# Retention attention, a routed expert layer and a gated convolution layer on one core: decodings spread evenly over the experts, routing's small products moved by a chunk, one product moved from GpSimd to VectorE

## The chip, the cores and the metric

The kernel runs on one core of one Trainium2 chip, in a single launch. The metric is the device time of that launch in microseconds (us). TensorE multiplies matrices, VectorE and ScalarE (DVE and ACT in the rows) move and change data, GpSimd (POOL) does some products and issues the gathers, and SyncE (SP) only issues transfers. Each engine takes its own instructions strictly in the order in which they stand, and waits for the others by semaphores.

## The reference

Three layers follow one another on a batch of 2 sequences of 768 tokens, 8 heads of 64 (512 features together).

```python
# 1. attention with a decaying state, for each head h
state = gamma[h] * state + outer(k[t], v[t]);   y[t] = scale * q[t] @ state
# 2. one expert of 8 for each token, chosen in sequence
fresh = argmax(logits[b, s])
e = fresh if s == 0 or local_gate[b, s] < 0.5 else prev_e
out[b, s] = softmax(logits[b, s])[e] * (relu(x[b, s] @ w1[e]) @ w2[e])     # 512 -> 1024 -> 512
# 3. a gated layer with a convolution of 3 taps along the sequence
h = relu(x @ w_in);   conv = sum_k conv_w[k] * shifted(h, k)
out = (h * sigmoid(conv)) @ w_out                                          # 512 -> 1024 -> 512
```

The weights of layer 3 (`w_in`, `conv_w`, `w_out`) arrive as 64-bit floats; the rest is 32-bit.

## The kernel before

**Attention** runs over 12 chunks of 128 tokens (6 a sequence), the loop over `i` at the end of `tile_kernel`. A chunk is a fixed row of steps on TensorE: `a_Z` (the state times q), `a_AV` (the masked scores times v), `a_S` (the next chunk's scores; VectorE then masks them into `A`), `a_U` (the state's update), `a_X` (the transposition of the result, with the router's logits) and `a_store`. The inputs of a chunk are loaded three chunks ahead by SyncE and scaled two ahead by GpSimd.

**Routing** decides which tokens go to which expert. It works on groups of chunks (`GROUPS`: three of 3, one of 2, one of 1) and has five parts, a generator `route(g)` that `part(g)` moves on by one: (1) seven small VectorE operations, (2) a transposition and a running maximum, (3) transpositions back and the one-hot matrix `OH`, (4) counting products and the slot rows `sl`, (5) products that put each token's number into its expert's slot (a region of the bank `state`, which `a_U` also writes). In the loop, `due` is the group that ended a chunk ago and `late` the one that ended two ago. `first_gather` fetches the tokens of expert 0's first 128 slots (`x0`) as soon as they are final: `floor0` fills up expert 0's first 128 slots after chunk 9 (`FIRST`), so that later tokens go to the second half.

**The experts** (`moe`). An expert has up to 256 slots. To keep 32-bit accuracy, each operand is split into a high and a low part, and three products replace one; VectorE and ScalarE split the weights unit by unit (`split_unit`: 128x1024, cast `whi` on ScalarE, difference `wlo` on VectorE), eight units an expert, some ten units ahead of their use. Experts 1 to 6 run as `L1` (first product, 4 steps `dt`), `T` (transposition of the next expert's tokens) and `L2` (second product, 4 steps `j`). The first and the last expert run as two halves of 128 slots, `alone`: 8 steps of the first product (f = 0, 1), after each f a `relu` into `hr` and a transposition back (`back(f)`), then 8 steps `ft` of the second. The caller puts work between the steps, numbered n.

**Decoding.** The 64-bit weights of layer 3 are turned into 32-bit ones while the experts run: 16 decodings of 128x512. `dec_first` has ScalarE read the raw tile `draw` (2 buffers) into `dmf` (magnitude and fraction; L217 and L218). `dec_second` has VectorE do five operations (L220 to L226) and GpSimd two (L228, L229), and then issues the load for the decoding after next (`dec_load`). `dec_first` first finishes what is open. The tile `dmf` and the tile `hr` of `alone` share one tag with two buffers (`tag="ow", bufs=2`). `MORE` gives experts 2, 3 and 4 three decodings each; expert 0 has one, experts 1, 5 and 6 two each, and the last one's second part stands in expert 7's first half, at n == 2.

**Layer 3** (`moe2`) alternates `h2` (first product of 386 columns, 12 products each block of 128 features, then `conv` on ScalarE, VectorE and GpSimd) and `o2` (second product).

Everything is emitted in program order (`manual_schedule`): no scheduler moves it.

Of the kernel before, what the change touches and what calls it, by code (L numbers as in the profile page):

```python
# [22 lines left out]
E = 8  # L23
# [11 lines left out]
FIRST = 9  # L35
# [11 lines left out]
MORE = (2, 3, 4)  # L47
# [13 lines left out]
def _consts():  # L61

    if _CONST:
# [24 lines left out]
        "floor0": np.broadcast_to(P * (np.arange(E) == 0), (P, E)),  # L88
        "floor1": np.broadcast_to(P * (np.arange(E) == E - 1), (P, E)),
# [12 lines left out]
def tile_kernel(ctx: ExitStack, tc: tile.TileContext, consts, qk, kv, w1, w2, w_in, conv_w, w_out, out):  # L102
# [336 lines left out]
    def route(g):  # L439
# [49 lines left out]
        if b == FIRST:  # L489

            ve.tensor_tensor(out=c_, in0=end, in1=cv("floor0"), op=ALU.max)
        elif b == NC:


            up = small([P, E], "up8")
            ve.tensor_tensor(out=up, in0=end, in1=cv("thr"), op=ALU.is_gt)
            ve.scalar_tensor_tensor(out=up, in0=up, scalar=float(P), in1=end, op0=ALU.mult, op1=ALU.add)
            ve.tensor_tensor(out=c_, in0=up, in1=cv("floor1"), op=ALU.max)
        else:
            ve.tensor_copy(c_, end)  # L500
# [78 lines left out]
    def transposed(x, hi, lo):  # L579
        p_ = bank("a")  # L580
# [17 lines left out]
    def first_T():  # L598
        xs0[:] = [dp.tile([P, KD, P], F32R, name="xs0", tag=tag) for tag in ("ds", "df")]
        transposed(x0, *xs0)  # L600

    def moe(mo):
# [86 lines left out]
        def L1(e):  # L689
# [3 lines left out]
            for dt in range(KD):  # L693
                wh, wl = split[e * 8 + dt]
                if dt == 0:
                    dec_second(nc.gpsimd)
# [22 lines left out]
        def L2(e):  # L719
# [3 lines left out]
            for j in range(KF // 2):  # L723
                wh, wl = split[e * 8 + KD + j]
                if j == (0 if e in MORE else 1):
                    dec_second(nc.gpsimd)
                    if e in MORE:
                        dec_first(mo)
                elif j == 2:
                    next(rest, None)  # L730
                elif j == 3:
                    dec_second(nc.gpsimd)
                    dec_first(mo)
# [19 lines left out]
        g3, g4 = len(GROUPS) - 2, len(GROUPS) - 1  # L753
        next(first)
# [16 lines left out]
        for n, _ in enumerate(first):  # L771
# [4 lines left out]
            if n == 4:  # L776
                overflow(mo)
        for n, _ in enumerate(alone(0, 1, True)):
            if n == 4:
                dec_first(mo)  # L780
            elif n == 9:
# [14 lines left out]
        for n, _ in enumerate(alone(e, 0, False)):  # L796
            if n == 2:
                dec_second(nc.gpsimd)
# [150 lines left out]
    def moe2(fo):  # L949
# [30 lines left out]
        def conv(c, ft, pb):  # L980
# [13 lines left out]
            nc.gpsimd.tensor_tensor(out=sg, in0=sg, in1=tap[1], op=ALU.mult)  # L994
# [77 lines left out]
    with tc.manual_schedule():  # L1072
# [22 lines left out]
        for i in range(NT):  # L1095
# [14 lines left out]
            part(late)  # L1110
# [4 lines left out]
            a_scale_q(i + 2, nc.gpsimd)  # L1115
            if not last_tile:
                a_S(i + 1)
            part(due)
            part(late)
            if i == FIRST + 1:  # L1120
                first_gather()
            a_U(i)
# [21 lines left out]
            if last_tile:  # L1144
                part(due)
                first_T()
# [57 lines left out]
```

## Time and profile before

| | |
|---|---|
| device time, median of 3 runs | 442.8 us (442.79, 442.8, 444.75) |
| profiled execution: its time, its span | 438.87 us, 436.8 us |
| TensorE busy | 404.5 us, 93% |
| VectorE, ScalarE, GpSimd busy | 296.2, 238.7, 164.5 us |
| mean granted TensorE clock | 0.975 of full speed |

How to read it: the span goes from the first to the last instruction of the profiled execution, and its own time is 2 us above that. In the table of stretches, a row names a stretch in us from the span's start, its length, the busy time and the number of instructions of each engine, the granted clock (1.00 is full speed, 0.50 half) and the share of the 16 DMA engines. In the table of waits, a row names the engine and instruction that waited, who released it, the sum, the number of times and the longest.

### The profile page before, as it was taken

The page shows a single profiled execution, that of the slowest core. Times are in us where ns is not written, and L with a number is a line of the kernel's source. Part 1 is how long each engine was busy: PE and PEld are TensorE (multiplying, and loading weights), DVE is VectorE, ACT ScalarE, POOL GpSimd, SP SyncE. Part 2 cuts the span into 40 slices and gives each one's busy share as a digit, 9 for nine tenths or more (in the row PEclk, how much of TensorE's full clock was granted, in tenths as well). Part 3 has the DMA queues.
Part 4 walks back from the last instruction along what each step waited for, and adds up shares of the span by engine and source line. Part 5 has one row for each costly group of instructions (what it writes and reads, how often), then busy time and mean ns, then how long its engine had stood idle before and what let it go on. Part 6 is the DMA issues. An engine that isn't in the chain of part 4 may idle for free.

```text
span 436.8 us, 7275 instructions
## 1 busy us (share of the span) xinstructions
PE 404.5 (93%) x2771; PEld 348.5 (80%) x2771; DVE 296.2 (68%) x485; ACT 238.7 (55%) x444; POOL 164.5 (38%) x143
## 2 busy tenths in 40 slices
PE   7998887899999995998979999969999999999996
PEld 3876675679989884896958987649987979998976
DVE  2377775649997959779797773576991633994250
ACT  2455542557666447285375752657865635883341
POOL 4644430210436425464464432503950300552030
PEclk9999998999999996999989999989999999999999
DMA  8999983477878768777697701311301001001001
GB/s 294 319 330 368 347 322 122 122 263 215 285 248 287 262 208 281 220 235 244 227 321 237 278 0 48 122 49 48 102 20 50 24 26 49 2 0 43 30 0 72
DMA packets 27974, 73.36 MB, mean 168 GB/s; under 512 B 2977, under 2 KB 3361, under 8 KB 27938
## 3 DMA queue, kind: packets, MB, share of 16 engines
q1 hardware_dynamic: 17490, 47.32, 31.8%
q0 software_dynamic: 4256, 14.68, 11.2%
q10 hardware_dynamic: 6192, 10.88, 6.7%
q8 instruction: 22, 0.36, 0.3%
q14 instruction: 14, 0.11, 0.1%
HBM read 62.39 MB, written 10.49 MB: 167 GB/s over the span
## 4 chain that ended last, share of the span: by engine, by line
PE 40%; DVE 23%; DMA 16%; issue 8%; ACT 7%; POOL 5%; SPq 0%; POOLq 0%; ACTq 0%; DVEq 0%
PE c L1022 11%; DVE wlo L185 6%; PE b L970 6%; DMA x<-scr,perm 6%; PE c L740 5%; DMA draw<-in_moe_w_out_dram 4%; PE rt L970 3%; DVE cs L989 3%; DVE gl L999 3%; ACT whi L177 2%; PE x L400 2%; PE sc L341 2%; POOL dmf L228 2%; POOL wdec L229 2%; PE xp L371 2%
## 5 line engine op out<-in xcount | busy, mean ns | idle before, releaser
L185 DVE TENSOR_TENSOR wlo<-raw,whi 128x1024 fp32r<-128x1024 f32 x64 | 85.1, 1347 | 26.9 <-ACT whi L177 26.6
L177 ACT CAST whi<-raw 128x1024 fp32r<-128x1024 f32 x64 | 66.5, 1055 | 23.6 <-PE c L740 14.5
L994 POOL TENSOR_TENSOR sg<-sg,hs 128x384 f32<-128x384 f32 x32 | 37.4, 1169 | 92.1 <-ACT sg L993 92.0
L228 POOL TENSOR_TENSOR dmf<-dmf,ds 128x512 f32<-128x512 f32 x16 | 29.9, 1867 | 93.9 <-DVE ds L226 65.9
L989 DVE SCALAR_TENSOR_TENSOR cs<-hs,cw,cs 128x384 f32<-128x384 f32 x64 | 43.9, 687 | 30.8 <-ACT cs L987 29.6
L740 PE MATMUL c<-whi,hh 128*128 128x512 f32 x96 | 40.2, 419 | 7.0 <-ACT hh L711 7.0
L740 PE MATMUL c<-wlo,hh 128*128 128x512 f32 x96 | 39.6, 412 | 0.0
L999 DVE TENSOR_TENSOR gl<-sg,gh 128x384 fp32r<-128x384 f32 x32 | 34.4, 1076 | 4.6 <-ACT gh L998 4.6
L1022 PE MATMUL c<-whi,gh 128*128 128x512 f32 x88 | 35.1, 399 | 0.8 <-ACT os L1036 0.8
L970 PE MATMUL b<-x,whi 128*128 128x386 f32 x168 | 35.8, 344 | 0.0
L1022 PE MATMUL c<-whi,gl 128*128 128x512 f32 x88 | 35.0, 397 | 0.1
L740 PE MATMUL c<-whi,hl 128*128 128x512 f32 x96 | 31.6, 412 | 3.6 <-DVE hl L712 3.6
L1022 PE MATMUL c<-wlo,gh 128*128 128x512 f32 x88 | 34.7, 394 | 0.0
L970 PEld LDWEIGHTS b<-x,whi 128*128 128x128 f32 x168 | 30.6, 194 | 0.1
L740 PEld LDWEIGHTS c<-whi,hh 128*128 128x128 f32 x96 | 19.3, 201 | 11.6 <-ACT hh L711 7.5
L229 POOL TENSOR_TENSOR wdec<-dmf 128x512 f32<-128x512 f32 x16 | 27.6, 1727 | 1.3
L706 PE MATMUL b<-xsh,wlo 128*128 128x256 f32 x96 | 27.1, 283 | 0.0
L706 PE MATMUL b<-xsh,whi 128*128 128x256 f32 x96 | 27.0, 281 | 0.0
L706 PE MATMUL b<-xsl,whi 128*128 128x256 f32 x96 | 26.8, 279 | 0.0
L740 PEld LDWEIGHTS c<-whi,hl 128*128 128x128 f32 x96 | 18.7, 199 | 9.3 <-DVE hl L712 5.6
L217 ACT ACTIVATE dmf<-draw 128x512 f32<-128x512 f32 x16 | 10.8, 676 | 27.8 <-DMA draw<-in_moe_w_out_dram 16.9
L610 POOL DMA_INDIRECT xg<-scr,permi x15 | 16.8, 1122 | 23.9 <-DVE nbi L541 13.7
(212 smaller groups left out, 1017.4 us busy)
## 6 DMA issues: line engine op xcount, KB each, us to landing
raw<-in_moe_w_dram SPq DMA_DIRECT2D x64, 512.0 KB, 5.1
qk<-in_qk_dram SPq DMA_DIRECT2D x11, 512.0 KB, 6.7
kv<-in_kv_dram SPq DMA_DIRECT2D x11, 512.0 KB, 5.3
scr<-ys ACTq DMA_DIRECT2D x16, 256.0 KB, 4.2
draw<-in_moe_w_out_dram POOLq DMA_DIRECT2D x8, 512.0 KB, 4.4
draw<-in_moe_w_in_dram POOLq DMA_DIRECT2D x6, 512.0 KB, 5.3
scr<-xo ACTq DMA_DIRECT2D x11, 256.0 KB, 6.6
out_dram<-os ACTq DMA_DIRECT2D x11, 256.0 KB, 2.0
```

Of the source, the lines that this page charges most:

```text
L177: nc.scalar.copy(hi, raw[u])
L185: engine.tensor_tensor(out=lo, in0=t, in1=hi.bitcast(F32), op=ALU.subtract)
L228: nc.gpsimd.tensor_tensor(out=f, in0=f, in1=s.bitcast(F32), op=ALU.mult)
L229: nc.gpsimd.tensor_tensor(out=out, in0=f, in1=a.bitcast(F32), op=ALU.add)
L610: nc.gpsimd.indirect_dma_start(out=t, out_offset=None, in_=xrow, in_offset=bass.IndirectOffsetOnAxis(ap=permi[:, col:col + 1], axis=0))
L706: nc.tensor.matmul(o, lhsT=a[:, fs], rhs=b_[:, dt, :], start=(dt == 0 and n == 0 and ft % 2 == 0), stop=(dt == KD - 1 and n == 2), skip_gr ...
L740: nc.tensor.matmul(yp[t], lhsT=a[:, ft, t * P:(t + 1) * P], rhs=b_[:, ws], start=(ft == 0 and a is hh and b_ is wh), stop=(ft == KF - 1 an ...
L970: nc.tensor.matmul(pb[:, 0:WN], lhsT=split[u_in + dt][wi][:, fs], rhs=x_[dt // 2][:, dt % 2, :], start=(n == 0), stop=(n == 3 * KD - 1))
L989: nc.vector.scalar_tensor_tensor(out=cs, in0=tap[j], scalar=cw[:, j, ft:ft + 1], in1=cs, op0=ALU.mult, op1=ALU.add)
L994: nc.gpsimd.tensor_tensor(out=sg, in0=sg, in1=tap[1], op=ALU.mult)
L999: nc.vector.tensor_tensor(out=gl, in0=sg, in1=gh.bitcast(F32), op=ALU.subtract)
L1022: nc.tensor.matmul(ops[t][:, 0:n_], lhsT=a[:, ts_], rhs=b_[:, ws], start=(ft == 0 and n == 0), stop=(ft == KF - 1 and n == 2))
```

## The change

Five things are done. (1) Decodings go to a schedule of two an expert: three start in expert 0 (the first in its first half, into the tiles `dmag` and `df`), two in each of the experts 1 to 6, and the last in expert 7's first half, at n == 6, with its second part at n == 13. (2) Their loads are issued by SyncE, the queue of the experts' weights, instead of GpSimd. (3) Routing's parts 2, 4 and 5 stand later in the loop: part 2 behind `a_U`, part 4 behind `a_AV`, part 5 one chunk later; the last two groups' parts are interleaved anew with expert 0's first steps. (4) `FIRST` becomes 6: expert 0's first 128 slots take tokens of the first sequence alone, `first_gather` stands in chunk 8 instead of 10, and the transposition of `x0` (`first_T`) stands before the last chunk's `a_X` and uses a bank of the scores. (5) The product of the sigmoid with h (L994) goes from GpSimd to VectorE.

```diff
-FIRST = 9
+FIRST = NC
-MORE = (2, 3, 4)
...
-        if b == FIRST:
-            ve.tensor_tensor(out=c_, in0=end, in1=cv("floor0"), op=ALU.max)
-        elif b == NC:
+        if b == NC:
...
-            ve.tensor_tensor(out=c_, in0=up, in1=cv("floor1"), op=ALU.max)
+            ve.tensor_tensor(out=c_, in0=up, in1=cv("floor"), op=ALU.max)
...
-        transposed(x0, *xs0)
+        transposed(x0, *xs0, sc2[:, 0])
...
                 if dt == 0:
-                    dec_second(nc.gpsimd)
+                    dec_second()
...
-                if j == (0 if e in MORE else 1):
-                    dec_second(nc.gpsimd)
-                    if e in MORE:
-                        dec_first(mo)
+                if j == 1:
+                    dec_second()
                 elif j == 2:
                     next(rest, None)
                 elif j == 3:
-                    dec_second(nc.gpsimd)
                     dec_first(mo)
...
         next(first)
+        part(g3)
+        next(first)
         part(g4)
         part(g3)
...
+            if n == 7:
+                dec_first()
         for n, _ in enumerate(alone(0, 1, True)):
-            if n == 4:
+            if n in (3, 12):
                 dec_first(mo)
-            elif n == 9:
+            if n == 9:
...
         for n, _ in enumerate(alone(e, 0, False)):
-            if n == 2:
-                dec_second(nc.gpsimd)
+            if n == 6:
+                dec_first(mo)
+            if n == 13:
+                dec_second()
...
-            nc.gpsimd.tensor_tensor(out=sg, in0=sg, in1=tap[1], op=ALU.mult)
+            nc.vector.tensor_tensor(out=sg, in0=sg, in1=tap[1], op=ALU.mult)
...
             a_Z(i)
-            part(late)
             a_AV(i)
             if i in SPLIT_STEPS:
                 split_first()
             a_load_qk(i + 3)
             a_scale_q(i + 2, nc.gpsimd)
+            part(late)
             if not last_tile:
                 a_S(i + 1)
-            part(due)
-            part(late)
-            if i == FIRST + 1:
+            else:
+                part(due)
+                first_T()
+            part(ends.get(i - 2))
+            a_U(i)
+            if i == FIRST + 2:
                 first_gather()
-            a_U(i)
+            if not last_tile:
+                part(due)
```

The file of the changed kernel is two lines shorter here, so its line numbers are 2 lower up to routing, and up to 6 lower in the experts.

**Routing in the attention loop, on TensorE**, from the counting products (`rt<-cnt`) of the group that ends at chunk 6 or 9. Before, one chunk's products and scores, and then at once the slot products:

```order
L485 LDWEIGHTS sel
L485 MATMUL rt<-cnt,sel 128x24
L371 MATMUL xp<-A,kv 64x128 x8
L341 MATMUL sc<-qk 128x128 x8
L511 LDWEIGHTS sl
L511 MATMUL state<-OHT,sl 128x8
```

Now:

```order
L483 LDWEIGHTS sel
L483 MATMUL rt<-cnt,sel 128x24
L339 MATMUL sc<-qk 128x128 x8
L388 MATMUL state<-kv 64x64 x8
L398 MATMUL x<-xw,xT 128x137 x4
L357 MATMUL xp<-qk,Z_103 64x128 x8
L369 MATMUL xp<-A,kv 64x128 x8
L339 MATMUL sc<-qk 128x128 x8
L506 LDWEIGHTS sl
L506 MATMUL state<-OHT,sl 128x8
```

Between the counting products and the slot products that need VectorE's answer (`sl`) stand now five steps of a chunk and the next scores, and before only two steps.

**The loads of the decodings**, on GpSimd before, in the middle of the experts (`dmf`, `wdec`: a decoding's two GpSimd operations; `draw`: the load; `xg`: the gather of an expert's tokens):

```order
L228 TENSOR_TENSOR dmf<-dmf,ds 128x512
L229 TENSOR_TENSOR wdec_86<-dmf 128x512
L246 DMA draw<-in_moe_w_in_dram 128x1024
L610 DMA xg<-scr,permi 128x512 x2
L228 TENSOR_TENSOR dmf<-dmf,ds 128x512
L229 TENSOR_TENSOR wdec_86<-dmf 128x512
L246 DMA draw<-in_moe_w_in_dram 128x1024
```

Now they stand on SyncE, among the loads of the experts' weights (`raw`):

```order
L164 DMA raw<-in_moe_w_dram 128x1024
L244 DMA draw<-in_moe_w_in_dram 128x1024
L164 DMA raw<-in_moe_w_dram 128x1024 x3
L244 DMA draw<-in_moe_w_in_dram 128x1024
L166 DMA raw<-in_moe_w_dram 128x2x512 x4
L164 DMA raw<-in_moe_w_dram 128x1024 x2
L244 DMA draw<-in_moe_w_in_dram 128x1024
```

The load no longer stands behind the two GpSimd operations of the decoding that frees its buffer.

**Expert 7's first half, on VectorE.** Before (`wlo<-wdec`: splits of decoded weights; `dmf`, `ds`: the last decoding; `hl`: the low part of `back(0)` and then `back(1)`):

```order
L185 TENSOR_TENSOR wlo<-wdec_86,whi 128x1024
L220 TENSOR_SCALAR dmf<-dmf 128x512
L221 TENSOR_SCALAR dmf<-dmf 128x512
L223 TENSOR_SCALAR ds<-draw 128x512
L224 SCALAR_TENSOR_TENSOR dmf<-dmf,ds 128x512
L226 TENSOR_SCALAR ds<-dmf 128x512
L643 TENSOR_TENSOR hl<-a_981,hh 128x4x128
L643 TENSOR_TENSOR hl<-a_980,hh 128x4x128
```

Now:

```order
L183 TENSOR_TENSOR wlo<-wdec_86,whi 128x1024
L638 TENSOR_TENSOR hl<-a_988,hh 128x4x128
L218 TENSOR_SCALAR dmf<-dmf 128x512
L219 TENSOR_SCALAR dmf<-dmf 128x512
L221 TENSOR_SCALAR ds<-draw 128x512
L222 SCALAR_TENSOR_TENSOR dmf<-dmf,ds 128x512
L224 TENSOR_SCALAR ds<-dmf 128x512
L638 TENSOR_TENSOR hl<-a_989,hh 128x4x128
L218 TENSOR_SCALAR dmf<-dmf 128x512
```

The last decoding but one, which was the last before, now begins behind the low part of `back(0)`, and the last one behind that of `back(1)`.

## Rows read from the trace of the kernel before

**Rows 1.** Stretches of experts 1 to 6, T and L2: length, engines' busy us, clock, DMA.

```profile
114.90:126.70 11.80, 11.80 (x58) 9.93 (x57) 11.08 (x17) 8.44 (x12) 2.49 (x3) 1.00 0.85 286
138.10:150.40 12.30, 12.13 (x58) 9.83 (x57) 11.88 (x16) 9.27 (x14) 4.43 (x4) 1.00 0.76 258
161.80:183.30 21.50, 15.83 (x58) 12.23 (x57) 18.64 (x27) 12.40 (x18) 11.05 (x8) 0.76 0.75 249
194.70:208.60 13.90, 12.03 (x58) 9.80 (x57) 13.43 (x16) 8.12 (x13) 8.20 (x7) 1.00 0.73 230
220.00:236.60 16.60, 13.71 (x59) 10.87 (x57) 14.98 (x18) 10.32 (x15) 9.54 (x7) 0.90 0.86 295
248.00:259.80 11.80, 11.80 (x58) 9.89 (x57) 10.41 (x15) 6.86 (x10) 3.14 (x2) 1.00 0.12 45
```

**Rows 2.** Waits of ScalarE, the two on the decodings' loads.

```profile
ACT dmf L217 <- DMA draw<-in_moe_w_out_dram: 16.9, 4, 6.1
ACT dmf L217 <- DMA draw<-in_moe_w_in_dram: 9.3, 1, 9.3
```

**Rows 3.** Instructions in order of time, end of expert 2, GpSimd and ScalarE.

```profile
147.97 2.12 POOL L228 TENSOR_TENSOR dmf<-dmf,ds 128x512 f32<-128x512 f32 x1 [7.49 <-DVE ds L226]
152.28 0.60 POOL L246 DMA_DIRECT2D draw<-in_moe_w_in_dram  x1
158.24 0.68 ACT L217 ACTIVATE dmf<-draw 128x512 f32<-128x512 f32 x1 [9.29 <-DMA draw<-in_moe_w_in_dram]
```

**Rows 4.** The page's DMA issues: count, KB, median us from issue to landing.

```profile
draw<-in_moe_w_out_dram POOLq DMA_DIRECT2D x8, 512.0 KB, 4.4
draw<-in_moe_w_in_dram SPq DMA_DIRECT2D x2, 512.0 KB, 8.1
```

**Rows 5.** Stretches of chunks 6 and 7, and of expert 0's two halves.

```profile
36.40:50.60 14.20, 10.55 (x162) 8.62 (x162) 12.94 (x25) 6.49 (x18) 5.89 (x5) 1.00 0.97 376
70.30:79.10 8.80, 7.24 (x36) 4.40 (x35) 4.63 (x25) 1.67 (x4) 0.00 (x0) 0.81 0.08 30
89.50:103.60 14.10, 13.67 (x66) 10.44 (x65) 8.23 (x10) 10.51 (x15) 1.89 (x2) 1.00 0.70 224
```

**Rows 6.** Waits of TensorE on routing and on the first gathered tokens.

```profile
PE state L511 <- DVE sl L506: 2.0, 1, 2.0
PE state L390 <- DVE perm L594: 1.4, 1, 1.4
PE rt L480 <- DVE OH L476: 1.3, 2, 0.9
PE rt L464 <- DVE code L460: 1.2, 2, 0.7
PE b L651 <- ACT xs L584: 0.8, 1, 0.8
```

**Rows 7.** Instructions in order of time, expert 7's first half.

```profile
262.18 0.42 DVE L220 TENSOR_SCALAR dmf<-dmf 128x512 f32<-128x512 f32 x1
264.16 0.43 DVE L226 TENSOR_SCALAR ds<-dmf 128x512 int32<-128x512 int32 x1
265.21 0.69 DVE L643 TENSOR_TENSOR hl<-a,hh 128x512 fp32r<-128x512 f32 x1 [0.62 <-ACT hh L642]
266.05 0.60 ACT L662 ACTIVATE hr<-b 128x512 f32<-128x512 f32 x1 [0.87 <-PE b L651]
266.11 1.28 POOL L229 TENSOR_TENSOR wdec<-dmf 128x512 f32<-128x512 f32 x1
266.70 0.42 PEld L639 LDWEIGHTS a<-C,hr 128*128 128x128 f32 x4 [0.49 <-ACT hr L662]
```

**Rows 8.** Layer 3: durations ns min/median/max of two lines; one block in the chain.

```profile
L989 DVE SCALAR_TENSOR_TENSOR cs<-hs,cw,cs x64: 603/619/1684, 298.9 to 418.1; 128x384 f32<-128x384 f32 x64
L999 DVE TENSOR_TENSOR gl<-sg,gh x32: 544/1224/1384, 305.1 to 422.3; 128x384 fp32r<-128x384 f32 x32
337.44 2.12 PE b L970 x12
```

More of the change, by code (lines that the diff above doesn't have):

```diff
@@ L87, in _consts @@
         "row": pid[:, None] + P * np.arange(KF)[None, :],
-        "floor0": np.broadcast_to(P * (np.arange(E) == 0), (P, E)),
-        "floor1": np.broadcast_to(P * (np.arange(E) == E - 1), (P, E)),
+        "floor": np.broadcast_to(P * (np.arange(E) % (E - 1) == 0), (P, E)),
         "thr": np.broadcast_to(np.where(np.arange(E) == E - 1, P, 2 ** 20), (P, E)),
@@ L576, in route_rest, with transposed @@
         yield
-    def transposed(x, hi, lo):
-        p_ = bank("a")
+    def transposed(x, hi, lo, p_=None):
+        p_ = bank("a") if p_ is None else p_
         for dt in range(KD):
@@ L1143, in tile_kernel @@
                 part(done)
-            if last_tile:
-                part(due)
-                first_T()
             if i == 2:
```

## The prediction, made before the changed kernel had run

> **What bounds the kernel now.** I read four views, in this order: the busy shares, the table of stretches, the waits of TensorE and ScalarE, and the instructions in order of time at the three places that the change touches. The shares say that TensorE does something in 93% of the span, so only time in which it stands idle or runs at the lower clock can be won. The stretches say where that time is. An expert's transposition and second product should always take the same time, and the reader is to see that it does not: 11.8 us for experts 1 and 6, but 12.3, 21.5, 13.9 and 16.6 us for experts 2 to 5 [rows 1]. Over 11.8 us these are 0.5 + 9.7 + 2.1 + 4.8 = 17.1 us. The first three of these four are the experts with three decodings, and the fourth follows on them. Part of it is the clock: 0.76 over 21.5 us is half speed for 10.3 us, 0.90 over 16.6 us half speed for 3.3 us, and half speed costs half of each.
>
> Why they are long stands in the waits. ScalarE waited 16.9 and 9.3 us for the loads of the decodings, five times in all [rows 2]. The end of expert 2 shows one: GpSimd starts the first of its two operations at 147.97, issues the load behind the second at 152.28, and ScalarE, which has nothing else to do in its order, waits 9.29 us until 158.24 [rows 3]. Behind that instruction stand the casts of the next weights, the stores, and the relu of expert 3; TensorE stops when expert 3's first product has no high part to go on with. So these stretches are bound by a load that is issued too late, for a decoding that stands too early, on an engine that works strictly in order.
>
> **Part 1 and 2: the schedule and the queue of the decodings.** With two decodings an expert, the load that a decoding frees is used by the decoding after next. From L2's second step to the next expert's third L1 step lie three quarters of an L2 and half an L1. An L2 with its T is 11.8 us, an L1 is what lies between the first two stretches, 138.1 - 126.7 = 11.4 us [rows 1], so the lead is about 8 + 5.7, nearly 14 us; the other load has more. The load also leaves earlier by GpSimd's two operations, 152.28 - 147.97 = 4.3 us [rows 3]. It needs 4.4 us from issue to landing on GpSimd's queue, and 8.1 us was measured for two on SyncE's queue, in the crowded attention stage [rows 4]. Either fits into 14 us. SyncE now waits for VectorE before each such load, and the weights' loads queue behind it; but each of these waits for a VectorE difference that stands behind the decoding anyway, so nothing new is late there. Experts 1 and 6, with two decodings each, run at 11.8 us today [rows 1], the first with full DMA traffic (0.85). I take the whole 17.1 us; bounded by 0 (the loads stay the limit) and 17.1.
>
> By a rule of the Trainium skill, "DMA: Bandwidth & Descriptors", section "Issuing engines are not separate DMA queues", transfers started by different engines interleave on the same 16 DMA engines, and starting them elsewhere saves only the issuing time. By it the new queue brings nothing by itself, and a load that lands late today could land as late tomorrow; the first rival below stands on the same point. The rows give it little room here, since 8.1 us on the busy queue is still under the lead.
>
> What this part adds: two decodings move into expert 0, from one to three. One costs VectorE 264.16 + 0.43 - 262.18 = 2.41 us [rows 7]. The first falls into a half in which VectorE is busy 8.23 of 14.1 us [rows 5] and is hidden. The other falls right ahead of expert 1, whose stretch keeps VectorE busy 11.08 of 11.80 us [rows 1]; it makes the low parts of expert 1 and perhaps 2 late. Bounds 0 and 4.8 us (both on the path); I take 2.0, most of one decoding, because VectorE has hardly any gap there.
>
> **A new wait, in expert 7.** Before, the last decoding's VectorE part runs at 262.18 to 264.59, in a gap ahead of the low part of `back(0)`, and its GpSimd part ends at 266.11 + 1.28 = 267.39, that is 2.80 us after VectorE [rows 7]. Now the last but one decoding has that VectorE part behind the low part of `back(0)`, which ends at 265.21 + 0.69 = 265.90. Then VectorE is done at 268.31 and GpSimd at 271.1. `dmf` and `hr` share two buffers. Of the two, the first half's `hr` leaves the one that the last decoding takes, so the second `hr` (f = 1) gets the one that GpSimd holds until 271.1. It started at 266.05 [rows 7], so it is 5.1 us late. Queued behind it on ScalarE is the high part of `back(1)`, and on TensorE the transposition of `hr`, which started at 266.70 [rows 7], with all that follows in order. Nothing covers it: + 5.1 us. Such a gap also drops the clock. After the 2.9 idle us of expert 5 (16.6 - 13.71) it was half for 3.3 us, a loss of 1.7; after expert 3's longer idle time half for 10.3, a loss of 5.2 [rows 1]. I take + 1.7, bounds 0 and 5.2. What follows (the store, the gathers, the last half) moves with it as a whole.
>
> **Part 3 and 4: routing and the first slots.** TensorE's waits for routing in the attention loop and for the first gathered tokens are 2.0 + 1.4 + 1.3 + 1.2 + 0.8 = 6.7 us [rows 6]. The slot products now have a whole chunk ahead of them, `OH` has a chunk's products, the reading of `perm` has left chunk 10, and the `x0` parts are ready before the last `a_X`. Not all of it is won: in chunks 6 and 7 VectorE is busy 12.94 of 14.2 us [rows 5], and the mask product that the next chunk needs now stands behind the counting operations, so some of the 2.0 comes back as a wait for `A`. I take 5.0. From below it is 0, since the DMA engines are at 0.97 in those chunks [rows 5] and a faster loop may wait for its inputs; from above 6.7 plus the 0.81 clock over 8.8 us (half for 3.3 us, a loss of 1.7) [rows 5], which a denser start of expert 0 might avoid: 8.4.
>
> **Part 5: the gate product.** A block of layer 3 costs TensorE 2.12 us [rows 8] and VectorE two L989 of 0.62 and one L999 of 1.22, together 2.46. L999 has the same form as the product that comes over, and alone it takes 0.54 (its minimum); the median is what it takes beside GpSimd's product [rows 8]. Without a GpSimd product VectorE would have 2 x 0.62 + 2 x 0.54 = 2.32 us, a little less than now. The chain at the end of each run of blocks gets shorter by the difference too. TensorE hides most of it, in long runs of `o2`. I take - 1.0; bounds - 2 and + 2.
>
> Against this stands the Trainium skill, "Perfetto Trace Analysis", section "Optimizing Scalar/DVE Operations": where VectorE is saturated, work may better go to ScalarE or even GpSimd, though the two share a read port and it might not help. The first half of that rule speaks for the order before, and the third rival is what it would do; the second half is what L999's minimum and median show here.
>
> **The sum.** Against the profiled execution: - 17.1 + 2.0 + 5.1 + 1.7 - 5.0 - 1.0 = - 14.3, so 438.87 becomes 424.6 us. The median of the runs lies 3.9 us above that execution; I take the same distance for the changed kernel, 442.8 - 14.3 = 428.5 us.
>
> **The rivals.**
> 1. The waits for loads stay in part: decodings evenly spread but VectorE full (18.64 busy us in expert 3's stretch [rows 1]) make the loads late again, or SyncE's order holds up the weights. For it: VectorE's high share in experts 1 and 2. Against it: experts 1 and 6 as they are. Half of the 17.1 lost: 437 us.
> 2. The wait in expert 7 is not on the path (the buffers go round otherwise than I read them): 5.1 + 1.7 less, 421.7 us. For it: the shortness of the place. Against it: ScalarE's `relu` has nothing between it and TensorE's next step.
> 3. Slower than before: VectorE becomes layer 3's bound. If L999 keeps 1.22 us and the product adds 0.54, a block needs 3.00 us against TensorE's 2.12. In 32 blocks that is 17.3 us over today's 2.46, and today's lag already uses the cover of the `o2` runs. With the gain of 1.0 gone it gives 428.5 + 18.3 = 447 us. It decides from 14.3 / 32 = 0.45 us more a block. Against it: the minimum of 0.54 [rows 8].
>
> **How the numbers follow.** The forecast has 0.63, the first rival 0.18, the second 0.12, the third 0.07. The forecast's own range is 422 to 436, from the bounds of its terms, which will not all fall on one side. The range that should hold 8 in 10 is 419 to 439. A measurement can tell 0.5% (2.2 us) from no change: faster than that 0.87 (the forecast, the second rival and most of the first), within it 0.05, slower 0.08.
>
> **What would show it.** In the profile after, T and L2 of experts 2 to 5 should take 11.8 to 13 us at full clock, and ScalarE should wait hardly at all for `draw`. Expert 7's second `hr` should wait for GpSimd, some 5 us, with a TensorE gap of that length. The first product of expert 0 should start about 5 us earlier than before, and L999's mean should be near 0.55 us. The prediction is wrong if expert 7 shows no gap, if stretches over 13 us remain in the middle experts, or if VectorE's time a block in layer 3 rises above 2.5 us.

## The result, and the profile after

The changed kernel takes 430.22 us (median of 4 runs, 430.10 to 432.69), the kernel before 442.80 (440.78 to 444.75): ratio 0.973, 95% interval 0.967 to 0.979. Run again on another chip it took 431.28 us against 440.74, ratio 0.971 (0.965 to 0.977). The profiled execution took 430.1 us, with a span of 428.3 us at a clock of 0.988. Forecast were 428.5 us.

Where the time went is seen from four stretches that cover both spans: the attention with expert 0, experts 1 to 6, expert 7 up to layer 3, and layer 3. First the table of stretches of the kernel before, then the same stretches of the changed one (columns as in [rows 1]):

```profile
5.70:103.60 97.90, 86.60 (x995) 68.70 (x995) 62.98 (x148) 49.99 (x116) 35.47 (x36) 0.98 0.79 277
103.60:259.90 156.30, 145.71 (x914) 130.82 (x913) 131.97 (x177) 90.72 (x127) 73.09 (x54) 0.96 0.74 241
259.90:292.80 32.90, 28.30 (x137) 21.31 (x136) 17.53 (x33) 17.24 (x34) 10.72 (x9) 0.99 0.23 72
292.80:436.70 143.90, 139.61 (x722) 126.34 (x720) 82.81 (x126) 80.74 (x168) 44.04 (x38) 0.99 0.10 35
```

```profile
5.70:104.70 99.00, 85.26 (x995) 68.78 (x995) 67.34 (x154) 51.08 (x120) 40.60 (x38) 0.98 0.78 275
104.70:248.00 143.30, 140.16 (x914) 127.37 (x913) 125.79 (x166) 89.33 (x123) 64.68 (x36) 1.00 0.77 261
248.00:287.60 39.60, 30.50 (x138) 23.17 (x136) 19.47 (x38) 18.30 (x36) 12.71 (x11) 0.91 0.20 60
287.60:428.30 140.70, 137.49 (x722) 125.25 (x720) 76.88 (x158) 81.04 (x168) 5.92 (x6) 1.00 0.11 36
```

The lengths differ by + 1.1, - 13.0, + 6.7 and - 3.2 us. So the gain is in the experts, as forecast; expert 7 gives back half of it, as forecast; the attention gives nothing, which was not.

T and L2 of experts 1 to 6 in the changed kernel, against [rows 1]:

```profile
116.00:130.20 14.20, 12.22 (x59) 9.93 (x58) 14.06 (x20) 8.53 (x13) 5.26 (x4) 1.00 0.81 264
141.50:155.00 13.50, 12.39 (x58) 9.91 (x57) 12.49 (x19) 10.47 (x15) 4.56 (x3) 1.00 0.77 253
166.20:178.50 12.30, 12.25 (x59) 9.97 (x58) 12.16 (x17) 6.94 (x10) 4.57 (x4) 1.00 0.75 266
189.80:201.60 11.80, 11.80 (x58) 9.89 (x57) 10.41 (x15) 6.85 (x10) 4.58 (x4) 1.00 0.81 270
212.90:224.80 11.90, 11.90 (x59) 9.98 (x58) 10.46 (x15) 6.91 (x10) 3.69 (x3) 1.00 0.73 245
236.10:247.90 11.80, 11.80 (x59) 9.88 (x58) 10.39 (x15) 6.88 (x10) 3.13 (x2) 1.00 0.14 47
```

Experts 3 to 6 run at their 11.8 to 12.3 us. Experts 1 and 2 have become longer, and expert 2's 13.50 us is over the 13 us that the prediction set as a sign of being wrong; VectorE has hardly a gap in expert 1's stretch (14.06 of 14.20 us). ScalarE's two waits of [rows 2], 26.2 us, are gone. Its waits for the experts' weights (`raw`) grew, from 4.1 to 12.2 us in eight pieces, but TensorE waits only 0.9 us for a high part (`hh`) in these experts. New is one wait for GpSimd, in expert 7:

```profile
ACT hr L657 <- POOL wdec L227: 4.7, 1, 4.7
```

In order of time that place reads as the prediction had it: GpSimd's product and sum of the last decoding but one, ScalarE's second `hr`, TensorE's transposition of it. Behind it the clock is low:

```profile
256.49 1.26 POOL L226 TENSOR_TENSOR dmf<-dmf,ds 128x512 f32<-128x512 f32 x1 [7.41 <-DVE ds L224]
257.83 1.26 POOL L227 TENSOR_TENSOR wdec<-dmf 128x512 f32<-128x512 f32 x1
259.12 0.60 ACT L657 ACTIVATE hr<-b 128x512 f32<-128x512 f32 x1 [4.68 <-POOL wdec L227]
...
259.77 1.12 PE L634 MATMUL a<-C,hr 128*128 128x128 f32 x4 [5.01 <-ACT hr L657]
```

```profile
259.70:268.00 8.30, 8.23 (x27) 6.75 (x28) 3.11 (x7) 0.60 (x2) 2.57 (x2) 0.67 0.00 0
```

In chunk 9 there is a wait that no one had foreseen. GpSimd runs the first gather and three scalings nearly without a gap, and VectorE's routing operations, 0.18 us elsewhere, last until GpSimd's end (55.47, 56.71, 57.95); TensorE waits 2.82 us for `code`:

```profile
52.45 1.94 POOL L590 DMA_INDIRECT x<-scr,perm  x1 [0.17 <-DMA kv<-in_kv_dram]
...
53.70 1.82 DVE L454 TENSOR_TENSOR eq<-LG,MX 128x24 f32<-128x24 f32 x1
...
54.42 1.05 POOL L326 TENSOR_TENSOR kv<-kv,C 128x512 f32<-128x512 f32 x1
55.45 1.26 POOL L320 TENSOR_TENSOR qk<-qk,tq 128x512 f32<-128x512 f32 x1
55.55 1.20 DVE L455 TENSOR_TENSOR eq<-eq,C 128x24 f32<-128x24 f32 x1
56.79 0.18 DVE L456 TENSOR_REDUCE m<-eq 128x3 f32<-128x24 f32 x1
56.91 1.04 POOL L326 TENSOR_TENSOR kv<-kv,C 128x512 f32<-128x512 f32 x1 [0.19 <-DMA kv<-in_kv_dram]
57.00 0.97 DVE L457 TENSOR_TENSOR m<-m,C 128x3 f32<-128x3 f32 x1
...
58.22 0.49 PE L462 MATMUL rt<-C,code 128*1 128x128 f32 x3 [2.82 <-DVE code L458]
```

The three long operations have two inputs. L456, which has one, ran in 0.18 us, but it began when one scaling had ended (56.71) and the next had hardly begun (56.91), so it tells nothing. The Trainium skill, "SBUF — State Buffer", section "SBUF: two separate sides", states that a VectorE operation with two SBUF inputs and a GpSimd operation that reads SBUF exclude each other for the whole instruction. The rows agree for the scalings.

TensorE's waits in the attention loop and expert 0 (30 to 105 us), against [rows 6]: the one for `code` has grown from 1.2 us, and two are new (for a scaled `qk` 0.2 us were waited before):

```profile
PE rt L462 <- DVE code L458: 3.6, 3, 2.8
PE sc L339 <- POOL qk L320: 1.8, 2, 1.2
PE c L398 <- DVE xs L580: 1.4, 1, 1.4
```

The first product of expert 0, which was to start some 5 us earlier, starts at 72.15 us, before at 71.82.

There is another new wait in expert 0's second half: TensorE waits 1.62 us for the first `hr`. In order of time, the third gather, VectorE's first store copy (`ys`) of that half, and the `hr` that stands behind it on ScalarE:

```profile
84.32 0.95 POOL L605 DMA_INDIRECT xg<-scr,permi  x1 [0.30 <-issue]
92.20 0.42 DVE L675 COPY ys<-c 128x256 f32<-128x256 f32 x1 [3.72 <-remote]
93.59 0.60 ACT L657 ACTIVATE hr<-b 128x512 f32<-128x512 f32 x1 [0.56 <-ACT ys L676]
```

The copy's input was ready at 88.42. The profile doesn't name who ended its wait (`remote`). By the times it is GpSimd, at the end of the branch for overflowing experts (`overflow`): there it waits until 91.70 for the third gather, which lands at 91.67. In the kernel before that gather had landed (88.94) before the copy's input was ready (89.68). In six profiles that tell the landing (this one, e1, e2, e3, e4, e12) the copy starts 0.53 us after it.

VectorE's three operations of a block in layer 3, against [rows 8]:

```profile
L987 DVE SCALAR_TENSOR_TENSOR cs<-hs,cw,cs 128x384 f32<-128x384 f32 x64 | 39.5, 619 | 33.8 <-ACT cs L985 32.6
L992 DVE TENSOR_TENSOR sg<-sg,hs 128x384 f32<-128x384 f32 x32 | 17.7, 553 | 2.7 <-ACT sg L991 2.7
L997 DVE TENSOR_TENSOR gl<-sg,gh 128x384 fp32r<-128x384 f32 x32 | 17.7, 552 | 0.4
```

With 32 operations more VectorE is busy 39.5 + 17.7 + 17.7 = 74.9 us here, where the two lines before cost 43.9 + 34.4 = 78.3 us (the third experiment shows the same busy times).

### The profile page after: what moved, and what is told of

It is laid out like the page before. It is cut to its first block, busy times and chain, and to the rows that moved or that the text cites. A ratio compares the mean times of both kernels' runs of the same rounds, so it can differ in the third digit from the quotient of the medians.

```text
span 428.3 us, 7286 instructions
## 1 busy us (share of the span) xinstructions
PE 397.7 (93%) x2771; PEld 345.9 (81%) x2771; DVE 290.4 (68%) x517; ACT 239.7 (56%) x444; POOL 125.0 (29%) x97
## 4 chain that ended last, share of the span: by engine, by line
PE 64%; DVE 18%; DMA 7%; issue 5%; ACT 3%; POOL 1%; another core or an unknown queue 1%; SPq 0%; ACTq 0%; DVEq 0%; POOLq 0%
PE c L1020 14%; PE b L968 10%; PE c L732 10%; DVE wlo L183 7%; PE rt L968 5%; PE b L701 4%; PE b L646 3%; DMA qk<-in_qk_dram 3%; DMA kv<-in_kv_dram 3%; PE rt L701 2%; PE state L701 2%; PE c L665 2%; DMA raw<-in_moe_w_dram 2%; PE sc L339 2%; PE xp L369 1%
## 5 line engine op out<-in xcount | busy, mean ns | idle before, releaser
L183 DVE TENSOR_TENSOR wlo<-raw,whi 128x1024 fp32r<-128x1024 f32 x64 | 83.0, 1311 | 17.0 <-ACT whi L175 16.9
L987 DVE SCALAR_TENSOR_TENSOR cs<-hs,cw,cs 128x384 f32<-128x384 f32 x64 | 39.5, 619 | 33.8 <-ACT cs L985 32.6
L732 PE MATMUL c<-whi,hh 128*128 128x512 f32 x96 | 38.0, 396 | 0.9 <-ACT hh L706 0.9
L732 PE MATMUL c<-wlo,hh 128*128 128x512 f32 x96 | 37.5, 390 | 0.0
L732 PE MATMUL c<-whi,hl 128*128 128x512 f32 x96 | 29.9, 393 | 2.2 <-DVE hl L707 2.2
L605 POOL DMA_INDIRECT xg<-scr,permi x15 | 21.1, 1405 | 26.8 <-DVE nbi L536 23.5
L701 PE MATMUL b<-xsl,whi 128*128 128x256 f32 x96 | 26.8, 280 | 0.0
L227 POOL TENSOR_TENSOR wdec<-dmf 128x512 f32<-128x512 f32 x15 | 26.3, 1752 | 1.2
L991 ACT ACTIVATE sg<-cs 128x384 f32<-128x384 f32 x32 | 16.7, 522 | 8.2 <-DVE gl L997 7.7
L344 DVE TENSOR_TENSOR A<-sc,C 128x1024 f32<-128x1024 f32 x12 | 14.6, 1220 | 9.7 <-PE sc L339 9.7
L732 PEld LDWEIGHTS c<-wlo,hh 128*128 128x128 f32 x96 | 18.1, 188 | 3.6
```

The costliest lines, as they stand in the source:

```text
L183: engine.tensor_tensor(out=lo, in0=t, in1=hi.bitcast(F32), op=ALU.subtract)
L227: nc.gpsimd.tensor_tensor(out=out, in0=f, in1=a.bitcast(F32), op=ALU.add)
L344: nc.vector.tensor_tensor(out=A_t[i], in0=sc.rearrange("p j (a t) -> p (j a) t", a=NP), in1=cv("mask").unsqueeze(1).to_broadcast([P, 2 * N ...
L605: nc.gpsimd.indirect_dma_start(out=t, out_offset=None, in_=xrow, in_offset=bass.IndirectOffsetOnAxis(ap=permi[:, col:col + 1], axis=0))
L701: nc.tensor.matmul(o, lhsT=a[:, fs], rhs=b_[:, dt, :], start=(dt == 0 and n == 0 and ft % 2 == 0), stop=(dt == KD - 1 and n == 2), skip_gr ...
L732: nc.tensor.matmul(yp[t], lhsT=a[:, ft, t * P:(t + 1) * P], rhs=b_[:, ws], start=(ft == 0 and a is hh and b_ is wh), stop=(ft == KF - 1 an ...
```

## Experiments

Twelve kernels ran, in four groups, each group beside the kernel before on one chip (there 438.6 to 440.9 us). Stage lengths are read from the starts and ends of TensorE's products in each run's profile: expert 1's first product, experts 1 to 6, expert 7 with the gathers up to layer 3, and the products of layer 3 (in brackets its first run of 144, which takes the changed kernel 25.45 us at full clock).

| kernel | median us (lowest to highest) | ratio to before, 95% | expert 1 starts | experts 1-6 | expert 7 | layer 3 |
|---|---|---|---|---|---|---|
| before | 442.80 (440.8-444.8) | | 103.6 | 156.3 | 32.9 | 140.4 (26.8) |
| changed | 430.22 (430.1-432.7) | 0.967-0.979 | 104.7 | 143.4 | 39.5 | 137.5 (25.45) |
| changed, again | 431.28 (426.6-435.9) | 0.965-0.977 | 104.6 | 143.4 | 39.0 | 139.1 (27.0) |
| e1 own buffer | 422.98 (419.7-429.5) | 0.956-0.965 | 103.4 | 143.3 | 32.8 | 139.1 (27.0) |
| e2 gather in chunk 10 | 433.34 (430.0-436.6) | 0.979-0.989 | 105.9 | 143.4 | 40.5 | 139.1 (27.0) |
| e3 gate on GpSimd | 433.50 (429.3-434.1) | 0.981-0.990 | 103.5 | 143.4 | 39.8 | 140.8 (26.2) |
| e4 routing as before | 431.70 (426.3-433.4) | 0.973-0.984 | 105.5 | 143.4 | 39.3 | 139.1 (27.0) |
| e6 loads on GpSimd's queue | 432.68 (431.0-436.1) | 0.977-0.988 | 102.8 | 146.2 | 40.0 | 139.1 (27.0) |
| e7 arithmetic later | 429.21 (426.8-430.6) | 0.968-0.978 | 102.8 | 143.1 | 39.5 | 139.1 (27.0) |
| e8 gather in chunk 9 | 426.51 (425.3-429.2) | 0.963-0.971 | 101.9 | 143.4 | 40.1 | 137.5 (25.45) |
| e9 three edits | 419.43 (417.7-422.0) | 0.950-0.959 | 99.4 | 143.2 | 32.8 | 139.1 (27.0) |
| e10 before, SyncE's queue | 432.16 (430.3-433.3) | 0.977-0.987 | 102.2 | 151.9 | 32.6 | 140.7 (26.1) |
| e11 decodings earlier | 429.03 (426.6-431.4) | 0.970-0.981 | 104.8 | 140.3 | 39.5 | 139.1 (27.0) |
| e12 best | 418.52 (416.7-422.0) | 0.949-0.961 | 101.0 | 140.0 | 32.9 | 139.1 (27.0) |

Executions of one kernel differ by several us. In the six profiles where nothing ahead of expert 1 was edited (both of the changed kernel, e1, e3, e6, e7) it starts between 102.8 and 104.7 us, and layer 3 differs by 1.6 us from one profile of the changed kernel to the other. Where an edit is worth less than 3 us, the stage that it touches is read, not the median, and a difference at expert 1's start under 2 us shows little.

**The changed kernel again**

> The changed kernel itself, unedited, as the measure for the three runs beside it. Its TensorE gap in expert 7 (5.0 us) and its wait for code in chunk 9 (2.8 us) come from the order of the instructions, so both theories expect them again. What differs from execution to execution is where TensorE falls to half clock: 430 us within 2 us, if the half clock comes at no other place than in chunk 9 and in expert 7.

Both waits came again, 5.0 and 2.8 us. The one in chunk 9 was reached in another way: a single operation of VectorE lasted 4.03 us, from 53.62 to 57.65, over three operations of GpSimd without a gap (54.34, 55.35 and 56.57 to 57.60).

```profile
53.62 4.03 DVE L454 TENSOR_TENSOR eq<-LG,MX 128x24 f32<-128x24 f32 x1
```

**e1, a buffer of its own** in expert 7:

```diff
-                    dec_first(mo)
+                    dec_first(mo if e < E - 2 else None)
```

> The changed kernel, but the last decoding but one (started in expert 6) gets a buffer of its own instead of one of the two that it shares with hr. Theory (the shared buffer holds up the second hr of expert 7): the gap of 5.0 us on TensorE at 254.8 goes, and with it the 2.6 us that the next 8 us lost at half clock; 430.2 - 4.9 - 2.6 + 0.5 for what is late next = 423. Rival A (GpSimd or ScalarE would be late there anyway, the buffer is only the last of several waits): the gap stays over 3 us, 429 to 431. Rival B (the gap goes, but the half clock comes at another place, as it did before the change ahead of layer 3): 425 to 427.

422.98 us, as the theory had it. Expert 7 falls from 39.5 to 32.8 us, what it took before the change, and no half clock is left in it:

```profile
246.50:279.50 33.00, 28.27 (x136) 21.20 (x135) 21.15 (x39) 17.96 (x36) 13.72 (x11) 1.00 0.23 72
```

So the wait was the shared buffer and nothing else. In this execution the start of layer 3 had a half clock (27.0 us); the unedited kernel shows it too in one of its two profiles, so the edit isn't shown to bring it.

**e2 and e8, the first gather in chunk 10 and in chunk 9**

```diff
-            if i == FIRST + 2:
+            if i == FIRST + 4:
                 first_gather()
```

That is e2; e8 has FIRST + 3.

> The changed kernel, but the first gather (GpSimd) is issued in chunk 10, as before the change, instead of chunk 8. Theory (GpSimd's gather and the scaling operations behind it run back to back beside VectorE's small routing operations of chunk 9, and each two-input operation of VectorE lasts until the GpSimd operation ends: 1.82, 1.20 and 0.97 us instead of 0.18): the three take 0.2 us each again, TensorE's wait of 2.8 us for code in chunk 9 falls under 1 us, the half clock after it goes; 3.5 to 4.5 us less, 426. Rival A (the attention loop is bound by its loads, and the time is lost again by the end of chunk 11): 429.5 to 430.5 with the wait moved to a load. Rival B (the gathered tokens come too late for the first transposition): 431 to 433.

> The changed kernel, but the first gather is issued in chunk 9, behind one scaling of the values and one of the queries, instead of in chunk 8 or (an earlier run) 10. Theory (the 3.4 us that VectorE's routing lost in chunk 9 came from GpSimd's pile behind the gather, and the gather takes some 6 us from its start to its landing, so it is still in time): the three operations take 0.2 us each, TensorE's wait for code in chunk 9 is under 1.2 us, no wait for x; 2 to 4 us less than the changed kernel. Rival A (the loop is bound by its loads): the wait goes and comes back as a wait for qk, same time within 1 us. Rival B (other routing operations collide with the gather in its new place): the same time.

In e2 the collision is gone: VectorE's L454, L455 and L457 take 0.18, 0.18 and 0.16 us (from 54.11 on). But the time was lost again, as rival B had it, and a little more: the gathered tokens arrive late. TensorE's waits of chunks 9 to 11 in e2, and in e8:

```profile
PE sc L577 <- DMA x<-scr,perm: 3.3, 1, 3.3
PE rt L462 <- DVE code L458: 0.7, 1, 0.7
```

```profile
PE rt L462 <- DVE code L458: 0.5, 1, 0.5
```

One chunk later instead of two has neither the wait for the tokens nor the long one for `code`. e8 took 426.51 us against 431.28 beside it. With this edit expert 1 starts at 101.9 us, and at 99.4 in e9, where nothing else ahead of it was edited; without it at 102.8 to 104.7. The mechanism is shown; its price is some 3 us, uncertain by the 2 us of that scatter.

**e3, the gate product back on GpSimd**

```diff
-            nc.vector.tensor_tensor(out=sg, in0=sg, in1=tap[1], op=ALU.mult)
+            nc.gpsimd.tensor_tensor(out=sg, in0=sg, in1=tap[1], op=ALU.mult)
```

> The changed kernel, but the gate product is on GpSimd as before. Theory (layer 3 gained 1.6 us by the product: 1.0 us in the first run of 72 products with gh and gl, 0.3 in the run of 30, 0.2 in the last; the other 1.3 us of layer 3's gain was the half clock at its start, which has to do with the waits of expert 7): 431.8, the product gl back at a median of 1.2 us. Rival A (it is worth nothing, TensorE hides it): 430.2. Rival B (all of layer 3's 2.9 us come from it): 433.

433.50 us, above the theory (431.8) and nearest to rival B (433). VectorE's two lines take again what they took before the change:

```profile
L987 DVE SCALAR_TENSOR_TENSOR cs<-hs,cw,cs 128x384 f32<-128x384 f32 x64 | 43.9, 687 | 30.7 <-ACT cs L985 29.6
L997 DVE TENSOR_TENSOR gl<-sg,gh 128x384 fp32r<-128x384 f32 x32 | 34.4, 1075 | 4.6 <-ACT gh L996 4.6
```

In this execution the first run of layer 3 had its full clock, and it still takes 26.2 us instead of 25.45; its last four blocks take 2.3 to 2.4 us each, where the changed kernel's take 2.1 to 2.3:

```profile
286.72:312.92 26.20, 26.20 (x148) 25.23 (x147) 21.35 (x39) 19.70 (x40) 14.55 (x14) 1.00 0.24 71
```

Behind the first run layer 3 takes 140.8 - 26.2 = 114.6 us with the product on GpSimd and 112.1 without (all kernels that have it on VectorE); in the kernel before, whose first run started at half clock, it was 113.6. So the product's move is worth more when layer 3 starts at full clock: 140.8 - 137.5 = 3.3 us, e3 against the changed kernel. When both start at half clock it is 140.4 - 139.1 = 1.3 us, the kernel before against the changed kernel's second profile. The half clock at the start seems to hide part of VectorE's delay: in the kernel before the last four blocks of that run take 2.1 to 2.3 us.

**e4, routing and first slots as before.** All of the change is undone but the decodings and the gate product: the groups' constants, the floors, the bank of the first transposition, and the order of the main loop.

```diff
-FIRST = NC
+FIRST = 9
...
-        transposed(x0, *xs0, sc2[:, 0])
+        transposed(x0, *xs0)
...
+            part(late)
             a_AV(i)
```

> The changed kernel, but with the routing, the first slots and the order of the attention loop as before; the decodings and the gate product as changed. Theory (by the two traces, the changed loop reaches the end of expert 0's first half 1.3 us earlier, not 5): 431.5. The prediction's term: 435.2. Rival (the changed loop is worth less than nothing, because its waits in chunk 9 and its half clock come on top): 428 to 430.

431.70 us, as the theory had it; expert 1 starts 0.8 us later than in the two profiles of the changed kernel and 1.9 later than the mean of the six (103.6). By these starts the routing's part is worth 1 to 2 us, not 5. Even less can't be excluded: e4's profile has a clock of 0.55 from 75 to 81 us, in expert 0's first half, where the kernel before has 0.81, and e4 ends that half 1.5 us later than the kernel before (91.2 against 89.7).

**e6, the decodings' loads back on GpSimd's queue, and e10, SyncE's queue in the kernel before**

```diff
-                    dec_second()
+                    dec_second(nc.gpsimd)
```

That is e6, in L1 and L2; e10 is the same edit the other way, at all four places of the kernel before.

> The changed kernel with the new schedule of the decodings, but in L1 and L2 their loads are issued by GpSimd's queue as before, behind the decoding's two operations. Theory (the schedule alone made the lead of some 14 us long enough, and the queue brings nothing): the same time as the changed kernel within 1 us, ScalarE waits for draw under 1 us in all. Rival (the queue is what ended the waits: issued behind GpSimd's operations, 4.3 us later, the loads are late again in the experts): 433 to 440, waits of ScalarE for draw of 3 us and more.

> The kernel before, with its own schedule (three decodings in experts 2 to 4), but the decodings' loads issued by SyncE's queue at all four places. It tells the queue from the schedule. Theory (the load of a third decoding is needed too soon after the one before it, whoever issues it; the queue is worth the 4.3 us by which SyncE issues earlier): ScalarE's waits for draw shrink from 26.2 to some 8 us and TensorE's stalls with them by a half to two thirds; 428 to 434, so with the new queue alone the larger part of the gain. Rival A (the schedule is what counts, the queue shares the same DMA engines and brings nothing): 438 to 441, waits of 20 us and more. Rival B (SyncE waits for VectorE before each load, the weights queue behind it, and come late): above 441, with waits of ScalarE for raw.

In e6 neither side is quite right: the waits are back, but small, and experts 1 to 6 are 2.8 us longer:

```profile
ACT dmf L215 <- DMA draw<-in_moe_w_out_dram: 7.8, 4, 3.2
ACT dmf L215 <- DMA draw<-in_moe_w_in_dram: 1.7, 1, 1.7
```

e10's time is the theory's, its reason is not. ScalarE waits for no such load at all, instead of 26.2 us. Yet experts 3 and 5 stay long (their T and L2: 19.0 and 16.3 us, where [rows 1] has 21.5 and 16.6), and experts 1 to 6 gain 4.4 us of 13. What TensorE waits for there has changed, first the kernel before, then e10:

```profile
PE c L740 <- ACT hh L711: 7.0, 2, 4.1
PE c L740 <- DVE hl L712: 3.6, 3, 1.9
```

```profile
PE c L740 <- DVE hl L712: 4.9, 3, 2.7
PE c L740 <- ACT hh L711: 2.3, 1, 2.3
```

So both are needed. The queue takes away the loads' lateness; with three decodings the low and high parts are late all the same. In expert 3's stretch VectorE is busy 16.10 of 19.00 us, and ScalarE waits 2.27 us in one piece for `raw`; which of the two holds up the other no run separates. Taken alone the schedule is the larger part: 156.3 to 146.2 in e6, against 151.9 in e10. By the Trainium skill, "DMA: Bandwidth & Descriptors", section "Issuing engines are not separate DMA queues", another queue saves only the issuing time. The transfer itself was indeed hardly faster (median 3.9 and 5.1 us on SyncE's queue in e10, 4.4 and 5.3 on GpSimd's before). Here the issuing time was the point: the instruction stood behind 4.3 us of GpSimd's work.

**e7, the first piece of the positions' arithmetic later, and e11, expert 0's decodings earlier**

```diff
-                elif dt == 1:
+                elif dt == 1 and e > 1:
                     next(rest, None)
```

```diff
+            if n == 8:
+                dec_second()
...
-            if n in (3, 12):
+            if n == 0:
+                dec_first(mo)
+            if n == 2:
+                dec_second()
+            if n == 12:
                 dec_first(mo)
```

The first is e7, in L1; the second e11, in the loops over the two halves of expert 0.

> The changed kernel, but the first piece of the positions' arithmetic (three VectorE operations, 2.5 us at 114.4) does not run in expert 1's first product, and the later pieces move on by one place. Theory (expert 1 waits 2.0 us for its low part because VectorE has two decodings and this piece in a row ahead of it): the wait for hl in expert 1's second product goes, and with it any half clock behind it; 1.5 to 3.5 us less than the changed kernel. Rival A (the wait moves to expert 2, where VectorE has as much to do): the same time within 1 us. Rival B (VectorE is late by more than this piece): the wait shrinks to about 1 us, 0.5 to 1.5 us less.

> The changed kernel, but in expert 0 the first two decodings are finished one place earlier each: the first one's VectorE part at the end of expert 0's first half, where VectorE is idle for 3.7 us, the second one's at the start of the second half. Between 104 and 114 us VectorE then has one decoding instead of two. Theory (this second decoding is what makes VectorE late in expert 1's second product): the wait of 2.0 us for hl there goes, with the half clock that can follow it, at the price of 0.4 us for the first hr of the second half; 1.5 to 3.5 us less than the changed kernel (431.3 on the chip of the last runs). Rival A (VectorE is late in expert 1 by the positions' arithmetic and the weights' differences as well): the wait shrinks but stays at 1 us or more, 0 to 1.5 us less. Rival B (the earlier decoding delays the casts and differences of expert 0's second half): up to 2 us more.

TensorE's waits in experts 1 to 6, first the changed kernel, then e7, then e11:

```profile
PE c L732 <- DVE hl L707: 2.2, 2, 2.0
PE c L732 <- ACT hh L706: 0.9, 1, 0.9
```

```profile
PE c L732 <- DVE hl L707: 3.1, 3, 1.6
```

```profile
PE c L732 <- DVE hl L707: 0.2, 1, 0.2
```

In e7 the wait went on to other experts, and the stage stays as it was (143.1 us): rival A; that its median is 2 us lower comes from elsewhere. In e11 the wait is gone and experts 1 to 6 take 140.3 us, 3.1 less: the second decoding of expert 0 was the cause (e11 moves the first too, but VectorE was done with that one at 94.9 us, well ahead of expert 1). e11's whole time, 429.03 us, can't be told from the changed kernel's: its expert 0 is no shorter (expert 1 starts at 104.8).

**e9, three edits (e1, e8, e7), and e12, the best (e1, e8, e11)**

> The changed kernel with three edits together: a buffer of its own for the last decoding but one, the first gather in chunk 9, the first piece of the positions' arithmetic one place later. Theory (they take away waits at three places that don't touch, so the gains add): own buffer 7 to 8 us, gather 4.8, positions 2 as measured one by one, so 431.3 - 14 = 417 against the changed kernel, with no wait of TensorE over 2.3 us left up to layer 3. Rival (a wait taken away moves the half clock to the next place, and part of the gain is lost again at the start of layer 3 or in expert 1): 419 to 422.

> The changed kernel with the buffer of its own (expert 7), the first gather in chunk 9 and the earlier decodings of expert 0 in place of the moved arithmetic. Theory (with the earlier decodings expert 1's wait for hl of 1.6 us is gone, and the arithmetic, back in its place, takes no time on the path): 2 to 3 us less than the three edits had, 416 to 418, waits of TensorE for hl under 1 us in all, experts 1 to 6 in 140.5 us or less. Rival (expert 1 is no longer late but expert 2 is, or expert 0's second half pays for it): 418.5 to 420.

e9 took 419.43 us, 2.4 above the sum of the gains (rival): e7 added nothing, and layer 3 has its half clock. e12 took 418.52: experts 1 to 6 are 3.2 us shorter, but expert 1 starts 1.6 us later. The first `hr` of expert 0's second half comes behind the earlier decoding (TensorE waits 2.1 us for `hr`, 1.2 in e9). The two can't be told apart by their medians; either beats the changed kernel by some 11 us and the kernel before by 4 to 5%.

## Why the prediction was right, term by term

- **The stalls of experts 2 to 5, - 17.1.** Right. Undisturbed, an expert takes 23.16 us from first product to first product (expert 6 in both traces), six take 139.0. Before they took 17.4 us more. With e11's edit only 1.3 is left. The mechanism was half of it: the loads' lateness was one cause; the other, which e10 shows by what remains, is that three decodings crowd an expert, and the first rival had named VectorE for it.
- **Two more decodings in expert 0, + 2.0, bounds 0 to 4.8.** The step held, the size was too small: 143.4 - 139.0 = 4.4 us, nearly all in experts 1 and 2, of which e11 takes back 3.1. I had priced one decoding's VectorE time; two stand in a row there. Expert 0's second half, from the end of the first half's products to expert 1, is 2.3 us longer as well (89.7 to 103.6 before, 88.4 to 104.7 after), but most of that isn't the decodings: in e4, which has them and the old loop, it is 0.4 us longer (91.2 to 105.5). With these 0.4 the decodings cost 4.8, the upper bound.
- **The wait in expert 7, + 5.1 and + 1.7.** Right in place, cause and size: 5.0 us of gap, 6.6 with the clock, and e1 takes off 6.7. It was read from which buffer is released when, which no row of the kernel before shows as a wait.
- **Routing and first slots, - 5.0.** This step failed. Four of the five waits of [rows 6] went, but the fifth, for `code`, grew from 1.2 to 3.6 us, and waits for `qk` and `xs` came. The first gather moved from 64.5 to 52.5, where GpSimd still scales and VectorE routes. I had counted the moved gather as an early start, not as an operation that VectorE's own have to wait for; by e8 the collision alone costs some 3. Expert 0's first half starts 0.3 us later than before and ends 1.3 earlier (89.7 to 88.4). Even these 1.3 are lost in the second half, whose first `ys` and `hr` wait for the third gather: it was issued 1.7 us later than before (82.60 to 84.32) and took longer to land. That wait is read from the trace; no run moves those gathers, so what it costs in the end is not shown. From the start to expert 1 it is + 1.1 us, the decodings' 0.4 included.
- **The gate product, - 1.0.** Right in sign, too small: 1.3 us with a half clock at the start of layer 3, 3.3 without (e3), beyond the bound of 2. GpSimd's product had lengthened the tap operations as well: 0.687 us on the mean where they take 0.619 now. [Rows 8] gave their median, 0.619, and not their mean. In layer 3's - 2.9 there is luck: this execution happened not to have the half clock at its start, and the next profile of the same kernel, which had it, is 1.6 us longer there.
- **The median above the execution, + 3.9.** Not carried over: the changed kernel's median is 0.1 us above its profiled execution. The sum against the execution was - 14.3 and came out as 438.87 to 430.1 = - 8.8. By stage the forecast was 6.1 us too good for the attention with expert 0 (- 5.0, measured + 1.1) and 2.1 for experts 1 to 6 (- 15.1 and - 13.0), right for expert 7 (+ 6.8 and + 6.7), and 2.2 too modest for layer 3 (- 1.0 and - 3.2). So 428.5 against 430.2 is closer than the terms were, by luck: against the execution the sum is 5.5 us off, and the distance between execution and median, which shrank from 3.9 to 0.1, gave most of it back.

## What to carry to other kernels

When an operation of GpSimd is moved, look at what VectorE does in the place it comes to: here a row of small routing operations with two inputs became as long as GpSimd's pile beside them. When a schedule shifts work past an allocation from a shared ring of buffers, follow who releases each buffer; one spare buffer was worth more here (6.7 us) than any other edit tried. And a late load has two owners: the queue that issues it late, and the engines that are too full to use it; moving it to another queue shows which.

## What the runs showed of the hardware

- A VectorE operation of 0.18 us lasted 4.03 us, over three GpSimd operations that followed one another without a gap. It need not: in the first profile of the same kernel the same operation ended with the first scaling (55.52 and 55.47), though the second followed at once, and in e1 one VectorE operation ended with each of the three. What decides it stays open.
- TensorE's half clock at the start of layer 3 (0.94 over 27.0 us instead of 1.00 over 25.4) came in ten of the fourteen profiles. The changed kernel shows both, with the same 2.2 us of idle time just ahead of it. What decides it stays open:

```profile
287.60:313.00 25.40, 25.40 (x147) 25.40 (x146) 21.34 (x48) 20.51 (x41) 5.92 (x6) 1.00 0.24 74
```

```profile
287.00:314.00 27.00, 27.00 (x148) 27.00 (x147) 21.86 (x49) 20.97 (x42) 5.92 (x6) 0.94 0.24 69
```

(the changed kernel's two profiled executions, start of layer 3).
